# Attention scores from four 64x64 products without the masked quarter, tokens' halves exchanged in every second head pair

## The chip, the cores and the metric

The kernel runs on one core of one Trainium2 chip. The metric is the device time of one launch in microseconds (us), less is better. Three runs of the kernel before took 798.5, 800.56 and 801.65 us.

## What is computed

A linear attention with decay, then two feed-forward layers. Per batch and head the attention goes over the tokens t in order:

```
cur   = (u * k_t) outer v_t
y_t   = r_t . (state + cur)
state = w * state + k_t outer v_t
```

There are 4 batches, 8 heads, 768 tokens and 48 numbers per head. Its output (3072 tokens of 384) goes through a layer of 8 experts, of which each token uses the one with the greatest gate, and through a gated layer: `(silu(x @ w_gate) * (x @ w_val)) @ w_out` with 1536 inner columns. All is fp32.

## The kernel before, in words

The attention works on 24 tiles of 128 tokens, six tiles to a batch (a sequence). Inside a tile the decay is divided out: with powers of w, `rdT` = r times w to the token's number and `kdT` = k divided by w to that number, both with the head's numbers on the partitions, and the *scores* are their product. Two heads share the 128 partitions, 64 each (48 used); so 8 heads are 4 pairs, counted by `q`, with `j` for the head in the pair.

The steps of a tile, and who does them:

- `scaled_k` (L454): GpSimd makes `ck` (k times u times r, L470 and L471), `kdT` (L473) and `kdc` (k decayed to the end of the tile, L475; not for the last tile of a sequence). In the first three tiles VectorE makes `ck` (L467, L468).
- `scaled_r` (L477): VectorE makes `rdT` (L484); for the last two tiles GpSimd does (L482). The loads of the tile three further on are issued here, on the queue of the sync engine (L356, L357, L361).
- `bonus` (L491): VectorE sums `ck` to `cb` (L496), and ScalarE writes for each head a diagonal matrix `dsb` with `cb` on the diagonal, from the identity (L500).
- `scores` (L503): TensorE makes for each head a 128x128 product (keys by queries) with 64 rows of the array (L513); the two heads of a pair use the two halves of the rows, and their results go to two PSUM buffers. VectorE copies them into `dsb`, only where the key comes before the query, by a mask (L517, one instruction for four heads).
- `state` (L525): TensorE makes the tile's addition to the state (L535), VectorE adds it (L545).
- `outputs` (L553): TensorE multiplies `v` by `dsb` (L561) and the state by `rdT` (L569; not for the first tile of a sequence); ScalarE copies the sum (L574).
- `rows_out` (L604): TensorE turns the result to one token per partition (L126, 64x64 products), ScalarE copies it, and a DMA stores it.

The order of the instructions is written out by hand for TensorE, VectorE, ScalarE and GpSimd (L624 on): in the round of tile i come the scores of i, then state and outputs of i-1 and the keys of i+2, then the rows of i-2. The routing of tokens to experts is cut into small steps of VectorE, which `advance` puts between the others (L583); its TensorE steps are issued where `advance(TENSOR)` stands.

Ahead of the loop, `powers` (L389) fills TensorE with five warm-up products `wu` (L397), all into one PSUM buffer, makes the powers of w on VectorE, and on ScalarE the four decay tables `we` (L411), which TensorE turns (L414) and ScalarE copies to `wk_tok` (L415); `kdc` needs that. `tables` (L417) has GpSimd clear the rest of the scratch buffer `yd_all` (L420), from which `carve` cuts the inputs' places. In GpSimd's order the keys of the tiles follow each other without anything else but these and, near the end, the splitting of expert weights (L1079).

After the attention the expert layer and the gated layer follow, mostly on TensorE; the change does not touch them. `sequential` (L779) is a slow branch for other decays than those that occur here; it is not taken.

Of the kernel before, what the change touches and what calls it, by code (L numbers as in the profile page):

```python
# [9 lines left out]
F32 = mybir.dt.float32  # L10
# [10 lines left out]
P = 128  # L21
# [17 lines left out]
def moe_kernel(ctx, tc, cst, small, tok, tr, u, w1, w2, m_gate, m_val, m_out, out):  # L39
# [281 lines left out]
    with ExitStack() as actx:  # L321
# [48 lines left out]
        load(0)  # L370
        nc.sync.dma_start(out=u_tok, in_=u.rearrange("(o h) d -> o h d", o=1).to_broadcast([P, H, D]))
        nc.sync.dma_start(out=cs, in_=cst)
        for i in range(1, NIO):
            load(i)
            load_v(i - 1)
# [13 lines left out]
        def powers():  # L389
            nc.vector.memset(ones, 1.0)  # L390
            nc.vector.memset(pw[:, :, 0:1], 1.0)
            for t in kdc_b:
                nc.gpsimd.memset(t[:, :, D:], 0.0)

            for i in range(WARM):
                wu = ps_m.tile([P, 512], F32, name="wu", tag="m")
                nc.tensor.matmul(  # L397
                    wu, lhsT=ones, rhs=ones.rearrange("p (o t) -> p o t", o=1).to_broadcast([P, 4, P]), start=True, stop=True
                )
            nc.vector.tensor_scalar(out=wc, in0=wp, scalar1=DECAY_MIN, scalar2=DECAY_MAX, op0=ALU.max, op1=ALU.min)  # L400
            for q in range(NP):
                nc.vector.tensor_tensor_scan(
                    out=pw[:, q, 1:], data0=wc[:, q : q + 1].to_broadcast([P, P]), data1=ones,
                    initial=1.0, op0=ALU.mult, op1=ALU.mult,
                )
            nc.scalar.copy(wr_ps, wrT)

            we = apool.tile([P, NP, P], F32, name="we", tag="yT")
            for q in range(NP):
                nc.vector.reciprocal(wkT[:, q, :], pw[:, q, 1:])  # L410
                nc.scalar.mul(we[:, q, :], wkT[:, q, :], pw[:, q, P : P + 1])  # L411
            pst = ps_m.tile([P, NP, P], F32, name="pst", tag="m")
            for q in range(NP):
                nc.tensor.transpose(pst[:, q, :], we[:, q, :], ident)  # L414
            nc.scalar.copy(wk_tok, pst.rearrange("p q (j d) -> p (q j) d", j=2)[:, :, 0:D])  # L415
# [23 lines left out]
                )  # L439
            nc.gpsimd.tensor_copy(unit[:, :, D:], wg[:, :, 0:G])  # L440

        S = {}

        def inputs(i):
            t = io[i % NIO]
# [45 lines left out]
        def bonus(i):  # L491
            if i >= NTILE:
                return
            r_t, k_t, rT, kT, rdT, kdT, ck, kdc = S[i]
            cb = apool.tile([P, H], F32, name="cb")
            nc.vector.reduce_sum(cb, ck, axis=AX.X)  # L496

            dsb = apool.tile([P, H, P], F32, name="dsb", bufs=3)
            for h in [*range(0, H, 2), *range(1, H, 2)]:
                nc.scalar.mul(dsb[:, h, :], ident, cb[:, h : h + 1])  # L500
            S[i] = rdT, kdT, kdc, dsb, heads(io_v[i % NV], 64)

        def scores(i):  # L503
            rdT, kdT, kdc, dsb, v_t = S[i]

            if i == 1:
                both = ps_x.tile([P, 2, NP, P], F32, name="pss01", tag="x")
                pss = [both[:, j] for j in range(2)]
            else:
                pss = [ps_s.tile([P, NP, P], F32, name=f"pss{j}", tag="s") for j in range(2)]  # L510
            for q, j in itertools.product(range(NP), range(2)):
                p0 = 64 * j
                nc.tensor.matmul(  # L513
                    pss[j][:, q, :], lhsT=kdT[p0 : p0 + 64, q, :], rhs=rdT[p0 : p0 + 64, q, :], start=True, stop=True
                )
            for j in range(2):
                nc.vector.copy_predicated(  # L517
                    dsb.rearrange("p (q j) t -> p q j t", j=2)[:, :, j, :],
                    mask.bitcast(I32).rearrange("p (o t) -> p o t", o=1).to_broadcast([P, NP, P]),
                    pss[j],  # L520
                )
                advance()
                advance()
# [255 lines left out]
    def sequential(c):  # L779
# [11 lines left out]
        with tc.For_i(0, B) as b:  # L791
            nc.vector.memset(st, 0.0)
            with tc.For_i(0, NCH) as ch:
                i = b * NCH + ch
                rk = sq.tile([P, 2, NP, P], F32, name="sq_rk")
                nc.sync.dma_start(
                    out=rk.rearrange("p a q t -> p (a q t)"), in_=tr[bass.ds(i, 1)].rearrange("o p n -> (o p) n")
                )
                yT = sq.tile([P, NP, P], F32, name="sq_y")
                nc.vector.memset(yT, 0.0)  # L800
                with tc.For_i(0, P) as t:
                    kv = sq.tile([P, NP, D], F32, name="sq_kv")
                    for j in range(2):
                        nc.sync.dma_start(
                            out=kv[64 * j : 64 * j + 64],
                            in_=v_d[bass.ds(i, 1), j, bass.ds(t, 1), :, 0:D]
                            .rearrange("o a q d -> (o a) q d").to_broadcast([64, NP, D]),
                        )
                    r_t, k_t = (rk[:, n, :, bass.ds(t, 1)] for n in range(2))
                    nc.vector.tensor_tensor(out=kv, in0=kv, in1=bc(k_t), op=ALU.mult)  # L810
                    cur = sq.tile([P, NP, D], F32, name="sq_cur")
                    nc.vector.tensor_tensor(out=cur, in0=kv, in1=col(up), op=ALU.mult)
                    nc.vector.tensor_tensor(out=cur, in0=cur, in1=st, op=ALU.add)
                    nc.vector.tensor_tensor(out=cur, in0=cur, in1=bc(r_t), op=ALU.mult)
                    psy = ps_m.tile([P, NP], F32, name="sq_psy", tag="m")
                    for q in range(NP):
                        for p0 in (0, 64):
                            nc.tensor.matmul(
                                psy[p0 : p0 + D, q : q + 1], lhsT=cur[p0 : p0 + 64, q, :], rhs=ones[p0 : p0 + 64, :],
                                start=True, stop=True,  # L820
                            )
                    for p0 in (0, 64):
                        pr = slice(p0, p0 + D)
                        nc.vector.tensor_copy(yT[pr, :, bass.ds(t, 1)], psy[pr].rearrange("p (q o) -> p q o", o=1))
                    nc.vector.tensor_tensor(out=st, in0=st, in1=col(wp), op=ALU.mult)
                    nc.vector.tensor_tensor(out=st, in0=st, in1=kv, op=ALU.add)
                for _ in emit(
                    yT, x_d[bass.ds(i * P, P), :], lg[:, bass.ds(i, 1), :].rearrange("p o g -> p (o g)"), sq, ps_y
                ):
                    pass  # L830
# [662 lines left out]
def _layout(inputs):  # L1493
# [7 lines left out]
    def tokens(a, pad=0):  # L1501
        a = a.transpose(0, 2, 1, 3)
        if pad:
            a = np.concatenate([a, np.zeros(a.shape[:3] + (pad,), a.dtype)], axis=3)
        return a.reshape(b * n, P, -1)

    def pair_rows(a, fill):

# [48 lines left out]
```

## Time and profile before

| | |
|---|---|
| median of three runs | 800.56 us (798.5 to 801.65) |
| profiled execution | 798.91 us, its span 797.2 us |
| TensorE busy | 777.5 us, 98% of the span |
| VectorE busy | 498.1 us, 62% |
| ScalarE busy | 346.8 us, 44% |
| GpSimd busy | 220.2 us, 28% |

The span runs from the first to the last instruction of the profiled execution. The attention lies in the first 116 us or so. In the rows below PE is TensorE, DVE VectorE, ACT ScalarE, POOL GpSimd and SP the sync engine, whose rows here are issues of DMAs; L513 is line 513 of the kernel. Times count from the start of the span. An fp32 product of TensorE is recorded as two MATMUL records.

### The profile page before, as it was taken

Reading aid. Unit: us, or ns where it says so; the run is one execution under the profiler, and the core shown is the slowest. Engines: PE = TensorE matmul, PEld = TensorE weight load, DVE = VectorE, ACT = ScalarE, POOL = GpSimd, SP = SyncE. Lnnn points to the kernel's source line nnn. Section 1 sums busy time; section 2 is a strip of 40 time slices with the busy share of each in tenths; the row PEclk is TensorE's granted clock in tenths of the full one; section 3 lists DMA queues with packets and bytes.
Section 4 is the critical chain, followed back from the end, with each engine's and each line's share of the span. In section 5 each row is a group of like instructions: output and inputs, shape, how many; then the busy total and the mean of one; then the engine's idle time right before and its main releaser. Section 6 shows DMA issues by size and latency. Waiting matters only on the chain.

```text
span 797.2 us, 15589 instructions
## 1 busy us (share of the span) xinstructions
PE 777.5 (98%) x5982; PEld 713.3 (89%) x5983; DVE 498.1 (62%) x1041; ACT 346.8 (44%) x785; POOL 220.2 (28%) x213
## 2 busy tenths in 40 slices
PE   8989998999999999999999999999999999999997
PEld 4878888899999999988888888888888888899997
DVE  7889976889999899787553335334433543344543
ACT  5878873656656656654432223222212221122322
POOL 6999986545233322120002000100200020001000
PEclk9999999999999999999999999999999999999999
DMA  8999974867877784564201000000100000000000
GB/s 321 307 336 339 303 268 142 289 199 220 253 239 238 248 246 144 159 191 140 89 14 40 1 0 14 40 1 1 44 9 1 7 40 1 1 8 40 1 21 24
DMA packets 61860, 99.28 MB, mean 125 GB/s; under 512 B 5461, under 2 KB 48105, under 8 KB 61776
## 3 DMA queue, kind: packets, MB, share of 16 engines
q1 hardware_dynamic: 58320, 88.34, 34.0%
q0 software_dynamic: 3456, 9.85, 3.6%
q8 instruction: 49, 0.80, 0.4%
q14 instruction: 35, 0.29, 0.1%
HBM read 81.64 MB, written 16.53 MB: 123 GB/s over the span
## 4 chain that ended last, share of the span: by engine, by line
issue 54%; PE 29%; POOL 8%; DVE 5%; DMA 1%; ACT 1%; POOLq 0%; SPq 0%; DVEq 0%; ACTq 0%
PE ph L1209 10%; PE py L1209 9%; POOL out_dram L1381 2%; PE pss L513 1%; PE psy L561 1%; POOL kdT L473 1%; POOL kdc L475 1%; PE psy L569 1%; POOL ck L470 1%; PE pya L1209 1%; PE wu L397 1%; POOL ck L471 1%; DMA rw<-m 1%; PE pt L1176 1%; PE pha L1209 1%
## 5 line engine op out<-in xcount | busy, mean ns | idle before, releaser
L1405 PE MATMUL pg<-x,wh 128*128 128x512 f32 (+1 forms) x504 | 146.6, 359 | 0.0
L1410 DVE TENSOR_TENSOR hv<-pg,hv 128x512 f32<-128x512 f32 (+1 forms) x84 | 51.6, 615 | 141.5 <-ACT hv L1409 141.4
L1405 PE MATMUL pv<-x,wh 128*128 128x512 f32 (+1 forms) x504 | 137.7, 358 | 0.0
L1381 POOL DMA_INDIRECT out_dram<-ot,tokd x24 | 24.9, 1038 | 407.1 <-DVE ot L1380 403.4
L1409 ACT ACTIVATE hv<-pg 128x512 f32<-128x512 f32 (+1 forms) x84 | 45.0, 536 | 158.5 <-PE pg L1405 158.1
L968 ACT CAST hh<-hv 128x512 fp32r<-128x512 f32 (+1 forms) x84 | 47.0, 560 | 136.7 <-DVE hv L1411 136.7
L1405 PEld LDWEIGHTS pv<-x,wh 128*128 128x128 f32 x504 | 89.9, 188 | 13.9
L1405 PEld LDWEIGHTS pg<-x,wh 128*128 128x128 f32 x504 | 90.2, 188 | 11.3
L1372 PE MATMUL po<-wh,hl 128*128 128x384 f32 x288 | 97.1, 338 | 0.0
L1372 PE MATMUL po<-wl,hh 128*128 128x384 f32 x288 | 96.8, 336 | 0.0
L1372 PE MATMUL po<-wh,hh 128*128 128x384 f32 x288 | 96.8, 336 | 0.0
L1405 PE MATMUL pg<-x,wl 128*128 128x512 f32 (+1 forms) x252 | 90.3, 358 | 0.0
L1405 PE MATMUL pv<-x,wl 128*128 128x512 f32 (+1 forms) x252 | 90.3, 358 | 0.0
L1209 PE MATMUL ph<-x,w1h 128*128 128x416 f32 (+6 forms) x336 | 87.5, 341 | 0.0
L1209 PE MATMUL py<-h,w2h 128*128 128x416 f32 (+6 forms) x336 | 82.4, 341 | 0.0
L969 DVE TENSOR_TENSOR hl<-hv,hh 128x512 fp32r<-128x512 f32 (+1 forms) x84 | 51.7, 616 | 43.6 <-ACT hh L968 43.3
L1411 DVE TENSOR_TENSOR hv<-pv,hv 128x512 f32<-128x512 f32 (+1 forms) x84 | 51.7, 615 | 38.5 <-PE pv L1405 37.9
L500 ACT ACTIVATE dsb<-cs,cb 128x128 f32<-128x128 f32 x192 | 58.7, 390 | 16.2 <-DVE cb L496 16.0
L1209 PEld LDWEIGHTS ph<-x,w1h 128*128 128x128 f32 x336 | 61.5, 188 | 0.2
L1209 PEld LDWEIGHTS py<-h,w2h 128*128 128x128 f32 x336 | 60.7, 188 | 0.5 <-DVE h L1229 0.3
L1050 POOL TENSOR_TENSOR low<-low,exw 128x384 f32<-128x384 f32 x30 | 32.9, 1098 | 97.7 <-DVE exw L1046 74.2
L1209 PE MATMUL ph<-x,w1l 128*128 128x416 f32 (+6 forms) x168 | 58.4, 348 | 0.7 <-DVE h L1229 0.7
(237 smaller groups left out, 1498.9 us busy)
## 6 DMA issues: line engine op xcount, KB each, us to landing
r<-in_w_dram SPq DMA_DIRECT2D x64, 384.0 KB
yd_all<-in_tr_dram SPq DMA_DIRECT2D x24, 512.0 KB
yd_all<-in_tok_dram SPq DMA_DIRECT2D x24, 384.0 KB
rw<-m SPq DMA_DIRECT2D x36, 192.0 KB
yd_all<-in_tok_dram SPq DMA_DIRECT2D x24, 256.0 KB
m<-ab SPq DMA_DIRECT2D x30, 192.0 KB
x_d<-xt SPq DMA_DIRECT2D x24, 192.0 KB
cva<-in_w_gate_dram SPq DMA_DIRECT2D x10, 384.0 KB
```

What stands on the lines that cost most here:

```text
L397: nc.tensor.matmul(wu, lhsT=ones, rhs=ones.rearrange("p (o t) -> p o t", o=1).to_broadcast([P, 4, P]), start=True, stop=True)
L500: nc.scalar.mul(dsb[:, h, :], ident, cb[:, h : h + 1])
L968: first = nc.scalar.copy(hi, src)
L969: second = nc.vector.tensor_tensor(out=lo, in0=src, in1=hi.bitcast(F32), op=ALU.subtract)
L1050: nc.gpsimd.tensor_tensor(out=low, in0=low, in1=ex.bitcast(F32), op=ALU.mult)
L1209: nc.tensor.matmul(dst[:, 0:n], lhsT=a, rhs=b, start=start and t == 0, stop=stop and t == 2)
L1372: mm = nc.tensor.matmul(po[t], lhsT=a[:, t * P : (t + 1) * P], rhs=bb, start=(f == 0 and j == 0), stop=(f == KF2 - 1 and j == 2))
L1381: st = nc.gpsimd.indirect_dma_start(out=out[:, :], out_offset=bass.IndirectOffsetOnAxis(ap=tokd[:, i : i + 1].bitcast(U32), axis=0), in_=o ...
L1405: nc.tensor.matmul(dst, lhsT=a[:, fs], rhs=bb[:, q, :], start=(q == 0 and j == 0), stop=(q == KD - 1 and j == 2))
L1409: nc.scalar.activation(hv, pg, AF.Sigmoid)
L1410: nc.vector.tensor_tensor(out=hv, in0=pg, in1=hv, op=ALU.mult)
L1411: nc.vector.tensor_tensor(out=hv, in0=pv, in1=hv, op=ALU.mult)
```

## The change

The scores of a head are made from two products instead of one, with keys and queries cut in halves of 64 tokens: the first 64 keys by all 128 queries, and the last 64 keys by the last 64 queries. The last 64 keys by the first 64 queries, all masked, are left out. In every second pair of heads the halves of the keys change places among the partitions: the first 64 keys stand on partitions 64 to 127. The host lays out r, k and v of these pairs so, the decay table `we` of these pairs is written in two pieces, and the identity and the mask have a second form, loaded by three DMAs behind the constants. The score buffers are the same ones all the time, and the first four warm-up products write them.

```diff
         nc.sync.dma_start(out=cs, in_=cst)
+        both = carve(4 * P).rearrange("p (s m t) -> p m s t", s=2, t=P)
+        for to, of in ((slice(0, P),) * 2, (slice(0, 64), slice(64, P)), (slice(64, P), slice(0, 64))):
+            nc.sync.dma_start(
+                out=both[to, :, int(to != of), :], in_=cst[of, 0 : 2 * P].rearrange("p (m t) -> p m t", t=P)
+            )
+        idents, masks = both[:, 0], both[:, 1]
         for i in range(1, NIO):
             load(i)
...
+            pss_b.append([ps_s.tile([P, NP, P], F32, name=f"pss{j}", tag="s") for j in range(2)])
+            both = ps_x.tile([P, 2, NP, P], F32, name="pss01", tag="x")
+            pss_b.append([both[:, j] for j in range(2)])
             for i in range(WARM):
-                wu = ps_m.tile([P, 512], F32, name="wu", tag="m")
+                wu = pss_b[i // 2][i % 2].rearrange("p q t -> p (q t)") if i < 4 else ps_m.tile([P, 512], F32, name="wu", tag="m")
...
-                nc.scalar.mul(we[:, q, :], wkT[:, q, :], pw[:, q, P : P + 1])
+                for a in range(1 + q % 2):
+                    to, of = (slice(0, P),) * 2 if q % 2 == 0 else (slice(64 * a, 64 * a + 64), slice(64 - 64 * a, P - 64 * a))
+                    nc.scalar.mul(we[:, q, to], wkT[:, q, of], pw[:, q, P : P + 1])
...
-                nc.scalar.mul(dsb[:, h, :], ident, cb[:, h : h + 1])
+                nc.scalar.mul(dsb[:, h, :], idents[:, h // 2 % 2], cb[:, h : h + 1])
...
-            if i == 1:
-                both = ps_x.tile([P, 2, NP, P], F32, name="pss01", tag="x")
-                pss = [both[:, j] for j in range(2)]
-            else:
-                pss = [ps_s.tile([P, NP, P], F32, name=f"pss{j}", tag="s") for j in range(2)]
-            for q, j in itertools.product(range(NP), range(2)):
-                p0 = 64 * j
+            pss = pss_b[i == 1]
+            for q, a, j in itertools.product(range(NP), range(2), range(2)):
+                pr, at = slice(64 * j, 64 * j + 64), 64 * (a ^ q % 2)
                 nc.tensor.matmul(
-                    pss[j][:, q, :], lhsT=kdT[p0 : p0 + 64, q, :], rhs=rdT[p0 : p0 + 64, q, :], start=True, stop=True
+                    pss[j][at : at + 64, q, 64 * a :], lhsT=kdT[pr, q, 64 * a : 64 * a + 64], rhs=rdT[pr, q, 64 * a :],
+                    start=True, stop=True,
                 )
             for j in range(2):
                 nc.vector.copy_predicated(
-                    dsb.rearrange("p (q j) t -> p q j t", j=2)[:, :, j, :],
-                    mask.bitcast(I32).rearrange("p (o t) -> p o t", o=1).to_broadcast([P, NP, P]),
-                    pss[j],
+                    dsb.rearrange("p (o s j) t -> p o s j t", s=2, j=2)[:, :, :, j, :],
+                    masks.bitcast(I32).rearrange("p (o s) t -> p o s t", o=1).to_broadcast([P, NP // 2, 2, P]),
+                    pss[j].rearrange("p (o s) t -> p o s t", s=2),
                 )
...
-        return a.reshape(b * n, P, -1)
+        a = a.reshape(b * n, P, h // 4, 2, 2, -1)
+        return np.stack([a[:, :, :, 0], np.roll(a[:, :, :, 1], 64, axis=1)], axis=3).reshape(b * n, P, -1)
```

The branch `sequential` is rewritten to read the exchanged values.

## Rows read from the trace of the kernel before

**Rows 1.** Busy us (and instructions) of the engines by stretch, then clock, DMA, GB/s.

```profile
core 0: us, PE busy (x) PEld busy (x) DVE busy (x) ACT busy (x) POOL busy (x), PEclk, DMA share, GB/s
11.17:109.06 97.89, 90.19 (x2020) 80.83 (x2016) 86.72 (x243) 80.15 (x255) 95.67 (x94) 0.98 0.95 335
...
180.00:200.00 20.00, 20.00 (x110) 19.64 (x109) 19.55 (x35) 13.27 (x27) 9.66 (x9) 1.00 0.77 225
```

**Rows 2.** Waits of POOL from 11 to 109.1 us: total, times, longest.

```profile
POOL kdc L475 <- ACT yd_all L415: 2.6, 1, 2.6
POOL ck L470 <- DMA yd_all<-in_tok_dram: 0.3, 1, 0.3
```

**Rows 3.** Groups of POOL from 11 to 109.1 us: busy us, mean ns, idle before.

```profile
L473 POOL TENSOR_TENSOR kdT<-yd_all 128x512 f32<-128x512 f32 x23 | 29.4, 1277 | 0.0
...
L475 POOL TENSOR_TENSOR kdc<-yd_all 128x384 f32<-128x384 f32 x20 | 20.3, 1017 | 2.6 <-ACT yd_all L415 2.6
...
L420 POOL MEMSET yd_all<- 128x860 f32 x1 | 0.8, 821 | 0.0
```

**Rows 4.** POOL in order of time: start, us, instruction; tiles 6 and 12.

```profile
32.92 1.28 POOL L473 TENSOR_TENSOR kdT<-yd_all 128x512 f32<-128x512 f32 x1
...
57.41 1.27 POOL L473 TENSOR_TENSOR kdT<-yd_all 128x512 f32<-128x512 f32 x1
```

**Rows 5.** PE in order of time over one tile, from scores to scores.

```profile
27.73 1.16 PE L513 MATMUL pss<-rdT,kdT 64*128 64x128 f32 x16
28.82 0.69 PE L535 MATMUL pskv<-yd_all,kdc 128*64 128x64 f32 x16
29.33 1.05 PE L561 MATMUL psy<-dsb,yd_all 128*64 128x128 f32 x16
30.31 0.98 PE L569 MATMUL psy<-rdT,st 64*64 64x128 f32 x14
...
31.13 0.73 PE L126 MATMUL psx<-unit,yT 64*64 64x64 f32 x30
31.79 1.16 PE L513 MATMUL pss<-rdT,kdT 64*128 64x128 f32 x16
```

**Rows 6.** POOL and PE in order of time where the last scores start.

```profile
107.80 1.20 POOL L482 TENSOR_TENSOR rdT<-yd_all 128x512 f32<-128x512 f32 x1
...
109.06 1.16 PE L513 MATMUL pss<-rdT,kdT 64*128 64x128 f32 x16
```

**Rows 7.** Chain of waits from 1 to 13 us: start, us, what.

```profile
3.22 2.09 PE wu L397 x2
...
9.95 0.64 PE pst L414 x4
...
11.17 1.13 POOL kdc L475
```

**Rows 8.** Start of the kernel: ACT, DVE and POOL in order of time, and one stretch.

```profile
7.54 0.40 ACT L411 ACTIVATE we<-yd_all 128x128 f32<-128x128 f32 x1 [0.41 <-DVE yd_all L410]
...
10.88 0.57 DVE L467 TENSOR_TENSOR bank<-yd_all 128x384 f32<-128x384 f32 x1 [0.75 <-DMA yd_all<-in_tok_dram]
...
13.49 1.01 POOL L475 TENSOR_TENSOR kdc<-yd_all 128x384 f32<-128x384 f32 x1
...
7.00:20.00 13.00, 10.35 (x105) 7.12 (x104) 10.22 (x18) 7.86 (x27) 10.16 (x14) 0.87 1.03 403
```

**Rows 9.** Group of the masked copy: busy us, mean ns, idle before.

```profile
L517 DVE COPY_PREDICATED dsb<-cs,pss 128x512 f32<-128x512 int32 x48 | 33.0, 739 | 3.2 <-PE pss L513 3.2
```

**Rows 10.** Chain of waits from 55 to 120 us, its shares by line.

```profile
by line: PE pss L513 17.0%; PE psy L561 15.8%; PE psy L569 13.5%; PE psx L126 10.1%; PE pskv L535 8.7%; DVE dsb L517 6.6%; DVE p_oh L209 4.3%; issue 4.3%; DVE yd_all L133 2.1%; DVE sel L216 1.8%; PE bank L220 1.6%; DVE x L969 1.6%; DVE bank
```

**Rows 11.** Two stretches as in rows 1, and PE in order of time around the first.

```profile
14.40:17.80 3.40, 3.40 (x42) 2.85 (x40) 3.37 (x7) 1.38 (x5) 3.28 (x6) 0.51 1.04 396
57.00:60.40 3.40, 1.88 (x42) 1.69 (x41) 3.40 (x11) 1.25 (x4) 3.40 (x4) 1.00 0.86 286
...
13.59 0.60 PE L513 MATMUL pss<-rdT,kdT 64*128 64x128 f32 x6 [1.91 <-POOL kdT L473]
...
15.75 1.92 PE L561 MATMUL psy<-dsb,yd_all 128*64 128x128 f32 x16
```

More of the change, by code (lines that the diff above doesn't have):

```diff
@@ L440, in units @@
             nc.gpsimd.tensor_copy(unit[:, :, D:], wg[:, :, 0:G])
-        S = {}
+        S, pss_b = {}, []
         def inputs(i):
@@ L800, in sequential @@
                 nc.vector.memset(yT, 0.0)
[L801 to L816, printed above, removed]
-                        for p0 in (0, 64):
[L818 to L826, printed above, removed]
@@ new lines, in sequential @@
+                for a in range(2):
+                    with tc.For_i(0, 64) as s:
+                        t = s + 64 * a
+                        kv = sq.tile([P, NP, D], F32, name="sq_kv")
+                        for j, o in itertools.product(range(2), range(2)):
+                            nc.sync.dma_start(
+                                out=kv[64 * j : 64 * j + 64, o::2, :],
+                                in_=v_d[bass.ds(i, 1), j, bass.ds(s + 64 * (a ^ o), 1), o::2, 0:D]
+                                .rearrange("o a q d -> (o a) q d").to_broadcast([64, NP // 2, D]),
+                            )
+                        r_t, k_t = (rk[:, n, :, bass.ds(t, 1)] for n in range(2))
+                        nc.vector.tensor_tensor(out=kv, in0=kv, in1=bc(k_t), op=ALU.mult)
+                        cur = sq.tile([P, NP, D], F32, name="sq_cur")
+                        nc.vector.tensor_tensor(out=cur, in0=kv, in1=col(up), op=ALU.mult)
+                        nc.vector.tensor_tensor(out=cur, in0=cur, in1=st, op=ALU.add)
+                        nc.vector.tensor_tensor(out=cur, in0=cur, in1=bc(r_t), op=ALU.mult)
+                        psy = ps_m.tile([P, NP], F32, name="sq_psy", tag="m")
+                        for q in range(NP):
+                            for p0 in (0, 64):
+                                nc.tensor.matmul(
+                                    psy[p0 : p0 + D, q : q + 1], lhsT=cur[p0 : p0 + 64, q, :], rhs=ones[p0 : p0 + 64, :],
+                                    start=True, stop=True,
+                                )
+                        for p0 in (0, 64):
+                            pr = slice(p0, p0 + D)
+                            nc.vector.tensor_copy(yT[pr, :, bass.ds(t, 1)], psy[pr].rearrange("p (q o) -> p q o", o=1))
+                        nc.vector.tensor_tensor(out=st, in0=st, in1=col(wp), op=ALU.mult)
+                        nc.vector.tensor_tensor(out=st, in0=st, in1=kv, op=ALU.add)
```

## Prediction

> **What bounds the kernel now.** I read the stretch of the attention first, because only there does the change touch anything that runs. Busy time by engine [rows 1]: from 11.17 to 109.06 us GpSimd works 95.67 of 97.89 us, VectorE 86.72, TensorE 90.19 (its ends are modelled, so this overstates it), and the DMA engines are busy 0.95 of the time. From 180 us on TensorE works 20.00 of 20 us. So a microsecond won at the end of the attention is carried through to the end, and the question is which engine ends the attention. The list of GpSimd's waits in that stretch has two entries [rows 2]: 2.6 us at the very start, for the table of decays that ScalarE copies, and 0.3 us for one load. Everything else is its own work; its two costliest groups [rows 3] are 23 products for the keys of the scores at 1.277 us and 20 for the keys of the state at 1.017. The line of time shows the pace [rows 4]: from the keys of tile 6 at 32.92 us to those of tile 12 at 57.41 us are 24.49 us for six tiles, 4.08 us each, back to back.
>
> TensorE's line of time over one tile [rows 5] shows the same pace with no hole: scores at 27.73, next scores at 31.79, 4.06 us. But that is a full tile. The first tile of a sequence has no product with the state (L569, 0.82 us), the last has no L535 (0.51), so six tiles are 6 x 4.06 - 1.33 = 23.0 us on TensorE against 24.49 on GpSimd. GpSimd never waits for TensorE. So GpSimd is the floor of this stretch, and TensorE runs just under it. At the end of the stretch GpSimd's last decayed rows (107.80 us, 1.20 long) release the last scores at 109.06 [rows 6].
>
> **The change, part by part.** *Scores.* Now a tile has 16 TensorE records (two to a product), two beside each other, so 8 steps of 128 columns: 1.09 us from L513 to L535 [rows 5]. After it there are 32 records on four quarters of the array. A step of 128 columns costs 0.82/8 = 0.10 us (L569, 30.31 to 31.13, the same 64x64 form); a step of 64 columns on four quarters costs 0.66/8 = 0.08 (L126, 31.13 to 31.79) [rows 5]. Each quarter gets 4 long and 4 short steps: 0.40 + 0.32 = 0.72 us, 0.37 less. If the quarters of unequal length did not overlap by columns, it would be 8 long and 8 short steps, 1.46 us, 0.37 more. L126 runs the four quarters together, so I take 0.72.
>
> The Trainium skill, TensorE: Matmul & The Clock Gate, Part 3 ("The mechanism"), speaks against the full figure: matmuls start and end strictly in program order. By that the short products of one pair hold up the long ones of the next, which use the same quarters, and a tile would come to about 8 long steps, 0.82 us; the sum below would lose 0.1 us. The trace of before has no unequal products on which to see it.
>
> What is it worth? Over 23 tiles 0.37 us is hidden behind GpSimd: TensorE is merely done earlier and waits. Only the last scores, released by GpSimd at 109.06, lie on the path: **-0.3 us** (ends -0.37 and +0.37). The doubled records (768 become 1536) cost nothing beyond this; what hides them is GpSimd's 4.08 us per tile, and without that cover the cost is the upper end.
>
> *Warm-up products.* Five of them run at the start, each waiting for the one before, since all write the same buffer. The chain [rows 7] gives 2.09 us for the two records of the second one (3.22), and it leads on to the transpose (9.95) that makes the table for which GpSimd waits until 11.17. In the change the first four write four different score buffers, and none waits. What they need without the wait: 8 steps of 0.10 per 128 columns is 0.80 us for two records of 512 columns at full clock, some 1.6 to 1.7 at half, against 2.09. Three waits of about 0.4 and one of about 0.3 go; part of the won time is at the half clock and is worth less. I take **-1.0 us** for the start of GpSimd's chain. Ends: 0 (they follow each other as before), and -1.5, because ScalarE's last input of the transpose, now done at 7.94 (7.54 + 0.40), will be there at some 8.4 [rows 8].
>
> *Two more ScalarE instructions* in the table of decays, at most 0.40 each like the present four [rows 8]; one of them is the last of the row. They end before the warm-up does, and it hides them; without that cover they cost 0.4.
>
> *Three loads ahead of tile 1.* They carry 128 x 2 x 128 numbers twice, 262 KB; at the 403 GB/s of this stretch [rows 8] that is 0.65 us, and the DMA engines are full (share 1.03). On the sync queue everything behind them (the loads of tiles 1 and 2, the first values) is issued three issues later. VectorE waits for tile 1 until 10.88 already [rows 8]; that becomes 11.5, and its work for tiles 0 and 1 slides with it. GpSimd needs tile 1's keys at 13.49 [rows 8], two microseconds after that. But it will be a microsecond earlier and the loads 0.65 later; the DMA share of 0.95 leaves little to catch up with, and GpSimd already waits 0.3 for a load [rows 2]. So part of the 1.0 is given back as waits for loads: **+0.5 us** (ends 0 and +1.5, all that was won; if nothing was won at the start, +0.65).
>
> *The clearing of the scratch room.* GpSimd clears what is left of the scratch buffer, 860 columns in 0.821 us [rows 3]. The two new tables take 512 of them, so 348 are left: 0.33 us, **-0.5 us** in the saturated chain. Ends -0.5 and 0.
>
> *VectorE's masked copies*, 48 at 739 ns [rows 9], keep their 512 elements; mask and destination now have three free dimensions instead of two. I take 0; a price is in the rivals. *ScalarE's diagonals* read another table of the same shape: nothing. The loop for wide decays lies in a branch that is not taken.
>
> **The sum.** -1.0 + 0.5 - 0.5 - 0.3 = -1.3 us. The profiled execution took 798.91 us, of which 797.2 are the span and 1.7 lie around it, so it would become 797.6. The three runs shown have a median of 800.56, 1.65 above the profiled one; against that median I forecast **799.3 us**. A change under 0.5%, 4 us, can't be told from none here.
>
> **The rivals.** *A: TensorE is the bound, and every tile gains.* For it: the chain of waits from 55 to 120 us names the scores first, with 17.0% [rows 10]. Then 24 x 0.37 = 8.9 us go, 791.7. Against it: GpSimd's work does not shrink by this and it has no holes to fill [rows 2, 3]; TensorE follows it, it does not feed it. 6%.
>
> *B: VectorE becomes the bound (slower).* Place: the masked copy L517. VectorE has 97.89 - 86.72 = 11.2 us free in the stretch [rows 1], 0.23 us for each of 48 copies. From 0.97 us a copy on VectorE sets the pace, and from 1.06 us the loss passes 4 us. If the third dimension halves the rate, 1.48 us: 48 x 0.74 - 11.2 = 24 us, 825. For it: no row shows this form. Against it: the number of elements is the same. 4%.
>
> *C: the quarters do not overlap (the change doesn't do what it says).* At 1.46 us TensorE's full tile becomes 4.43 us and six tiles 6 x 4.43 - 1.33 = 25.25, against GpSimd's 24.49 [rows 4, 5]: 0.76 for each of four sequences and 0.37 for the last scores, +3.4, 804.0. It decides from scores of about 1.33 us. Against it: L126 overlaps. 4%.
>
> *D: the clock falls.* Between 14.4 and 17.8 us the granted clock was 0.51 on the mean, so the lower level, 1.2 GHz [rows 11], after TensorE had waited 1.91 us for the keys; L561 then took 1.92 us against 1.05 [rows 5, 11]. TensorE will wait more often now. For a fall near 106 us, with nothing to hide it, half of 3.4 us is lost, 1.7: 801.0. Against it: between 57 and 60.4 us TensorE worked only 1.88 of 3.40 us and the clock stayed at 1.00 [rows 11]. 6%.
>
> **How the numbers follow.** My case has 80%. Its lower end takes all gains: -1.5 - 0.5 - 0.37 = -2.4; its upper end none, with the late loads and the worse scores: 0.65 + 0.37 = +1.0. To both come 1.6 us, half the spread of the runs shown (798.5 to 801.65): 796.6 to 803.2, which takes in D as well. A, B and C lie outside. Faster by over 0.5% is A and the edge of my case, 0.07; slower by over 0.5% is B and, with scatter, part of C, 0.06; the rest, 0.87, is no difference.
>
> **What would show it.** Right: GpSimd's wait at the start ends near 10.2 us instead of 11.17; its chain still has no wait for TensorE, 4.08 us per tile; its clearing shows 348 columns and 0.33 us; TensorE gets waits for GpSimd's keys or rows that it does not have now; scores to L535 take 0.7 to 0.85 us; the last scores start near 108. Wrong: a mean of L517 over 0.97 us, scores over 1.1 us, GpSimd waiting for TensorE, waits for loads of more than 2 us in all, or a tile of GpSimd shorter than 4.08 us, which would make rival A possible.

## The result: slower by 0.85%, and the profile after

The kernel after took 807.33 us (median of six runs, 805.07 to 808.27); the kernel before, run beside it, 799.88 (six runs, 798.35 to 801.65). The ratio is 1.0085, with an interval of 1.0068 to 1.0102: about 7 us slower. The forecast was 799.3 us, with a range up to 803.2; it missed on the slow side. The profiled execution after took 805.59 us, its span 803.7, against 798.91 and 797.2 before.

**Where the time went.** The expert stage begins with the products of `pha`. Their first one, in order of time, stands at 118.04 us before and at 125.46 after (the first fence is before, the second after):

```profile
118.04 0.36 PE L1209 MATMUL pha<-x,w1l 128*128 128x256 f32 x1 [0.38 <-ACT lh L128]
```

```profile
125.46 0.36 PE L1219 MATMUL pha<-x,w1l 128*128 128x256 f32 x1 [0.37 <-ACT lh L128]
```

From there to the end of the span are 679.2 us before and 678.2 after. So all of the loss, 7.4 us, arises in the attention. Busy time by stretch in the kernel after, first the stretch of [rows 1], then three stretches of the attention (columns as in [rows 1]):

```profile
11.17:109.06 97.89, 81.80 (x2217) 73.18 (x2219) 82.58 (x230) 74.92 (x238) 91.51 (x91) 0.95 0.92 322
...
40.00:60.00 20.00, 15.69 (x481) 14.08 (x474) 15.95 (x48) 15.35 (x48) 19.61 (x20) 1.00 0.94 319
...
80.00:100.00 20.00, 17.80 (x501) 16.22 (x502) 16.00 (x43) 14.70 (x47) 16.82 (x17) 0.91 0.81 277
100.00:120.00 20.00, 15.06 (x385) 12.84 (x383) 13.97 (x51) 11.80 (x35) 14.88 (x13) 1.00 0.83 281
```

Every engine works less in the stretch from 11.17 to 109.06 us: TensorE 81.80 us for 90.19 before, and GpSimd 91.51 for 95.67. From 40 to 60 us GpSimd is still full, as forecast, while TensorE idles over 4 us; from 80 us on GpSimd has holes too. No engine is full all the way to the end, so none of them alone sets the pace; something delays them all.

**The waits of TensorE** from 20 to 118 us tell what. Before, there is one row of "issue" (the first fence); after, all of these rows and the longest of another kind stand in the second (us in total, times, longest):

```profile
PE psx L126 <- issue: 0.8, 2, 0.5
```

```profile
PE psx L126 <- issue: 5.6, 3, 2.9
PE pss L520 <- issue: 2.5, 5, 1.1
PE psy L569 <- issue: 2.2, 2, 2.0
PE psy L577 <- issue: 2.2, 2, 1.4
PE psy L569 <- ACT yT L582: 1.7, 2, 1.4
PE bank L178 <- issue: 0.5, 1, 0.5
...
```

"issue" means that the engine waited for nothing that the profile shows. That is 5.6 + 2.5 + 2.2 + 2.2 + 0.5 = 13.0 us after, against 0.8 before. The waits fall in the middle of groups whose data are all there. The longest, in order of time:

```profile
77.58 0.47 PEld L126 LDWEIGHTS psx<-unit,yT 64*64 64x64 f32 x13
...
77.69 0.50 PE L126 MATMUL psx<-unit,yT 64*64 64x64 f32 x11
...
78.54 1.26 POOL L484 TENSOR_TENSOR kdT<-yd_all 128x512 f32<-128x512 f32 x1
...
81.06 0.42 PEld L126 LDWEIGHTS psx<-unit,yT 64*64 64x64 f32 x19 [3.02 <-issue]
81.07 0.56 PE L126 MATMUL psx<-unit,yT 64*64 64x64 f32 x19 [2.88 <-issue]
```

The 32 weight loads of a tile's rows are cut after 13; the other 19 come 3 us later, with the same `yT` and the same `unit`. Their data are there, so what is missing must be the instructions themselves; the DMA queues bear this out. What the DMA queues carried from 78.69 to 79.65 us (packets, MB, share of 16 engines):

```profile
q1 hardware_dynamic: 166, 0.36, 102.2%
q8 instruction: 1, 0.02, 6.1%
```

Queue q8 carries instructions in packets of 16 KB; the count below shows that TensorE's are among them. This packet's record begins at 78.70 us and lasts 0.94; TensorE goes on at 81.07, 1.43 us after its end. In the 0.5 us ahead of it and in the 1.4 us behind it the queue view has no q8 packet, only data, with the DMA engines full. Packets that begin at 42.11, 47.40, 57.52, 100.20, 105.72 and 111.90 us are followed in the same way, 1.3 to 1.7 us after their end, by the ends of waits of 1.62, 1.15, 1.08, 2.01, 0.83 and 1.36 us. So end 11 of the 13 "issue" waits between 20 and 118 us; the other two are of 0.24 and 0.27 us. Over the whole execution q8 carries this (packets, MB, share):

```profile
q8 instruction: 52, 0.85, 0.4%
```

It was 49 packets and 0.80 MB before. The Trainium skill, TensorE: Matmul & The Clock Gate, Part 2 ("Step-by-step: what each phase is for"), speaks of the 64-byte MATMUL instruction. The trace agrees in size, for matmuls and weight loads together: the page counts 6366 matmuls and 6367 weight loads after against 5982 and 5983, 768 more in all, and 768 times 64 bytes is three packets of 16 KB.

**How the rest answers to the rows before.** GpSimd's work, its wait at the start, one tile of TensorE and VectorE's masked copies:

```profile
L484 POOL TENSOR_TENSOR kdT<-yd_all 128x512 f32<-128x512 f32 x23 | 29.3, 1275 | 0.0
L481 POOL TENSOR_TENSOR ck<-yd_all 128x384 f32<-128x384 f32 x21 | 21.1, 1006 | 2.9 <-DMA yd_all<-in_tok_dram 2.9
...
L486 POOL TENSOR_TENSOR kdc<-yd_all 128x384 f32<-128x384 f32 x20 | 20.8, 1040 | 2.5 <-PE pskv L543 1.3 <-ACT yd_all L426 1.2
...
L431 POOL MEMSET yd_all<- 128x348 f32 x1 | 0.4, 385 | 0.0
```

```profile
10.01 1.00 POOL L486 TENSOR_TENSOR kdc<-yd_all 128x384 f32<-128x384 f32 x1 [1.18 <-ACT yd_all L426]
```

```profile
24.85 0.90 PE L520 MATMUL pss<-rdT,kdT 64*64 64x128 f32 x32
25.68 0.69 PE L543 MATMUL pskv<-yd_all,kdc 128*64 128x64 f32 x16
```

```profile
L525 DVE COPY_PREDICATED dsb<-yd_all,pss 128x512 f32<-128x512 int32 x43 | 29.6, 733 | 9.8 <-PE pss L520 6.6 <-ACT xt L130 2.0 <-ACT lh L128 0.5
```

The scores take 25.68 - 24.85 = 0.83 us up to L543, where they took 1.09 [rows 5]. The start wait of GpSimd ends 1.16 us earlier [rows 7]. But GpSimd now waits 2.9 us for loads instead of 0.3, 1.7 of them from 79.8 us on, and 1.3 us for TensorE's state products (L543), which read the buffer `kdc` that it wants to write; that it never did [rows 2].

The last scores start at 115.27 us, 6.2 later than in [rows 6]. From 100 to 126 us the chain of waits has 20.9% "issue" and no piece of GpSimd at all. There the stalls lie on the path themselves:

```profile
99.95 0.54 PE psy L569 x9
100.49 2.01 issue
102.50 0.65 PE psy L569 x7
...
112.43 0.69 PE psy L577 x9
113.11 1.36 issue
114.47 0.54 PE psy L577 x6
```

**When it is lost** can be read from GpSimd's keys. Those of tile 17 (78.54 us after, shown above) start 0.10 us earlier than before; those of tile 23, the last, start 2.68 us later. The first two rows are before, the third is after:

```profile
78.64 1.27 POOL L473 TENSOR_TENSOR kdT<-yd_all 128x512 f32<-128x512 f32 x1
...
104.79 1.27 POOL L473 TENSOR_TENSOR kdT<-yd_all 128x512 f32<-128x512 f32 x1
```

```profile
107.47 1.27 POOL L484 TENSOR_TENSOR kdT<-yd_all 128x512 f32<-128x512 f32 x1
```

So the waits that end before 70 us, 4.8 of the 13.0, cost GpSimd's pace nothing, and up to there the added loads, the tables and the exchange have not set it back either. The 8.2 us of waits from 78.19 us on come together with the whole loss of 7.4.

Last, the granted clock. Near the start its stretch at 0.50 (second row), the lower level of 1.2 GHz, is longer than the one in [rows 11], 6.83 us for 3.40; by the keys of tile 17 that has cost GpSimd nothing. And the clock fell once more, right after the 2.9 us stall (first row):

```profile
81.64:85.05 3.41, 3.41 (x63) 3.26 (x65) 2.25 (x7) 3.04 (x10) 2.46 (x3) 0.50 0.58 169
13.37:20.20 6.83, 6.21 (x104) 5.64 (x106) 6.80 (x13) 3.59 (x12) 5.82 (x9) 0.50 1.04 398
```

### The profile page after: what moved, and what is told of

The parts are those of the page before. It is cut to its first block, busy times and chain, and to the rows that moved or that the text cites. A ratio compares the mean times of both kernels' runs of the same rounds, so it can differ in the third digit from the quotient of the medians.

```text
span 803.7 us, 16363 instructions
## 1 busy us (share of the span) xinstructions
PE 773.3 (96%) x6366; PEld 710.6 (88%) x6367; DVE 496.5 (62%) x1041; ACT 347.8 (43%) x787; POOL 220.3 (27%) x213
## 4 chain that ended last, share of the span: by engine, by line
issue 56%; PE 24%; DVE 8%; DMA 5%; POOL 4%; ACT 2%; SPq 1%; POOLq 0%; ACTq 0%; DVEq 0%
PE ph L1219 5%; PE py L1219 5%; PE psy L569 2%; POOL out_dram L1391 2%; PE psy L577 2%; PE pss L520 2%; PE pskv L543 1%; PE psx L126 1%; DMA m<-ab 1%; PE pya L1219 1%; DMA m<-x 1%; DVE ab L1063 1%; DMA rw<-m 1%; PE pha L1219 1%; DVE w2l L1089 1%
## 5 line engine op out<-in xcount | busy, mean ns | idle before, releaser
L511 ACT ACTIVATE dsb<-yd_all,cb 128x128 f32<-128x128 f32 x192 | 58.8, 393 | 12.4 <-DVE cb L507 12.2
```

The lines of the kernel that those rows point to most:

```text
L511: nc.scalar.mul(dsb[:, h, :], idents[:, h // 2 % 2], cb[:, h : h + 1])
```

## The experiments

The theory after this reading, called **program** below: TensorE has 768 more instructions and gets through them sooner, its next pieces of program queue behind data in full DMA engines, and it stalls. The rivals: the additional loads, tables and exchanged halves cost; or keeping the score buffers costs; or the form of the products does. All runs in one table. "Ratio" is to the kernel before of the same session; "issue" is TensorE's wait for nothing that the profile shows from 20 to 118 us; q8 the packets of program; the last column is the first product of `pha`. The last three columns are of the one profiled execution, which need not be a middle one: those of e4 (800.42 us, median 798.25) and e12 (805.58, median 802.96) are the longest of their runs, that of e13 (800.89, median 801.96) is among the shortest.

| run | ratio (interval) | issue, us | q8 | attention ends, us |
|---|---|---|---|---|
| before | 1 | 0.8 | 49 | 118.04 |
| after | 1.0085 (1.0068 to 1.0102) | 13.0 | 52 | 125.46 |
| after, again (e14) | 1.0082 (1.0061 to 1.0104) | 14.6 | 52 | 127.19 |
| after, rows by 8 (e1) | 1.0046 (1.0029 to 1.0064) | 0.5 | 49 | 123.35 |
| before, rows by 8 (e2) | 1.0083 (1.0054 to 1.0112) | 0 | 46 | 123.84 |
| before, scores split (e3) | 1.0157 (1.0129 to 1.0186) | 1.5 | 52 | 136.23 |
| before, three loads (e4) | 0.9994 (0.9978 to 1.0010) | 5.5 | 49 | 120.88 |
| after, fewer v loads (e5) | | 1.7 | | 117.14 |
| before, fewer v loads (e6) | | 0 | | 116.61 |
| after, rounded rows (e7) | 1.0004 (0.9991 to 1.0018) | 1.0 | 47 | 120.04 |
| before, empty instructions (e8) | 1.0002 (0.9990 to 1.0015) | 2.5 | 49 | 119.17 |
| before, spread warm-up (e9) | 0.9988 (0.9968 to 1.0009) | 6.6 | 49 | 122.66 |
| before, rounded rows (e10) | 0.9969 (0.9945 to 0.9994) | 0 | 44 | 117.44 |
| after, half split (e11) | 1.0076 (1.0052 to 1.0100) | 0.7 | 50 | 125.71 |
| before, quarters (e12) | 1.0052 (1.0032 to 1.0072) | 10.0 | 52 | 126.37 |
| before, quarters in odd tiles (e13) | 1.0054 (1.0034 to 1.0074) | 3.4 | 50 | 119.30 |

In the session of e9 to e11 the kernel before itself took 803.66 us (798.82 to 806.60), in all others 797.85 to 799.88.

The table can also be read execution by execution. In the eight with all loads, the rows of x by 16 products, and in each tile either whole or quartered scores (before, e8, e13, e4, e9, e12, after, e14), the waits are 0.8, 2.5, 3.4, 5.5, 6.6, 10.0, 13.0 and 14.6 us, and the attention ends at 118.04, 119.17, 119.30, 120.88, 122.66, 126.37, 125.46 and 127.19: nearly in step, whichever kernel it is.

**e1 and e2: the rows of x in half as many products.**

```diff
-        for q, (j, k) in itertools.product(range(NP), ((0, 0), (1, 1), (0, 1), (1, 0))):
-            pr, ts = slice(64 * j, 64 * j + 64), slice(64 * k, 64 * k + 64)
-            nc.tensor.matmul(psx[ts, j, q, :], lhsT=yT[pr, q, ts], rhs=unit[pr, q, :], start=True, stop=True)
+        for q, j in itertools.product(range(NP), range(2)):
+            pr = slice(64 * j, 64 * j + 64)
+            nc.tensor.matmul(psx[:, j, q, :], lhsT=yT[pr, q, :], rhs=unit[pr, q, :], start=True, stop=True)
```

> The changed kernel, but the rows of a tile (L126) are made by 8 products of 64x128 instead of 16 of 64x64, so TensorE's program has as many products per tile as before the change (48 instead of 56). Theory code: TensorE runs through its program faster than the next piece of it arrives, while the DMA engines are full; its waits for nothing that the profile shows, 13.0 us in the attention of the changed kernel and 0.8 before, fall under 2 us, and the time falls to 797 to 800.5 us. Theory loads (the three loads ahead of tile 1 delay what follows): the time stays at 805 to 808, GpSimd's waits for loads at about 2.9 us. Theory array (the 64x64 products themselves or the clock): 805 to 808.

> The kernel before with the rows of a tile made by 8 products instead of 16: 40 products per tile instead of 48. Theory code: the kernel before waits only 0.8 us for its program, so little is there to win: 798.5 to 801. The other theories say the same; a loss of over 1 us would price the form 64x128 in place of 64x64 for the rows.

The waits went (0.5 and 0 us), as the theory has it, but neither time came (e1 802.69 us, e2 804.71): both kernels pay for the form, 128 columns of weights for 64 streamed ones. In e2 the weight loads, grouped by form from 60 to 80 us (busy us, mean ns):

```profile
L126 PEld LDWEIGHTS psx<-unit,yT 64*128 64x128 f32 x75 | 4.6, 188 | 0.7 <-issue 0.5 <-ACT dsb L500 0.2
...
L569 PEld LDWEIGHTS psy<-rdT,st 64*64 64x64 f32 x48 | 2.5, 133 | 0.5 <-issue 0.3 <-DVE dsb L517 0.2
```

From the rows' first record to the next scores it is 0.94 us in e2 (64.71 to 65.65 us), and before it was 0.66 [rows 5], with twice as many products. The longer weight loads fit that; that they alone set the pace is not shown. TensorE became the bound in e2 (20.00 us busy of 20 between 40 and 60 us). The Trainium skill, TensorE: Matmul & The Clock Gate, Part 2 ("Step-by-step: what each phase is for"), has this rule: the time of a weight load scales with its columns, not with its rows. The two rows agree in direction (188 ns for 128 columns, 133 for 64); both have 64 rows, so they say nothing on that half of the rule. What the two runs show together: the same edit costs 0.8% before and gains about 0.4% after. They do not give the size of the stalls.

**e3: additional instructions in the kernel before**, each score product in two, by halves of the queries.

```diff
-                nc.tensor.matmul(
-                    pss[j][:, q, :], lhsT=kdT[p0 : p0 + 64, q, :], rhs=rdT[p0 : p0 + 64, q, :], start=True, stop=True
-                )
+                for ts in (slice(0, 64), slice(64, P)):
+                    nc.tensor.matmul(
+                        pss[j][:, q, ts], lhsT=kdT[p0 : p0 + 64, q, :], rhs=rdT[p0 : p0 + 64, q, ts], start=True, stop=True
+                    )
```

> The kernel before with each product of the scores split by queries into two of 64 columns: 56 products per tile as in the changed kernel, but the form 64x128, the masked quarter, the layout and the loads of before; TensorE's work grows by about 0.05 us a tile. Theory code: waits of 8 to 14 us in TensorE's stream and 804 to 809 us. Theory loads: 799 to 801. Theory array: 799 to 801.5.

Longer by more than forecast (811.71 us), and not by stalls: each weight of 128 columns is loaded twice, and the scores take a median of 1.98 us up to the next group instead of 1.09, not 0.05 more. It waits 1.5 us for its program although it has as many instructions as after. So the number alone does not do it. Two reasons are possible, and the run does not separate them: TensorE, held up by its products, needs the next piece later; and the data queue's share from 20 to 118 us is 81.7% here, not 88.2%.

**e4: the three loads and the smaller clearing alone**, in the kernel before.

```diff
+        both = carve(4 * P).rearrange("p (s m t) -> p m s t", s=2, t=P)
+        for to, of in ((slice(0, P),) * 2, (slice(0, 64), slice(64, P)), (slice(64, P), slice(0, 64))):
+            nc.sync.dma_start(
+                out=both[to, :, int(to != of), :], in_=cst[of, 0 : 2 * P].rearrange("p (m t) -> p m t", t=P)
+            )
```

> The kernel before with the three loads of the second identity and mask behind the constants, unused (and 512 columns less for GpSimd to clear). Theory code: 799.5 to 801.5, no new wait of TensorE. Theory loads: 804 to 808, with GpSimd waiting for loads about 2.9 us. Theory array: 800.

No change in the median. Yet its profiled execution, the longest of twelve, has 5.5 us of the same waits:

```profile
PE pskv L540 <- issue: 3.7, 2, 2.0
...
PE psx L126 <- issue: 1.0, 1, 1.0
PE psy L566 <- issue: 0.8, 2, 0.5
```

So the stalls are no new thing of this change. They were not free here either: the attention of this execution ends 2.84 us later than in that of before, although GpSimd's last keys start 0.64 us earlier (104.15 us for 104.79), and one stall of 2.01 us lies on the chain that ends last, from 98 to 122 us:

```profile
101.67 2.01 issue
```

**e5 and e6: the same programs with less DMA.** From tile 4 on no values are loaded, so the outputs are computed from old ones; the tokens then crowd on few experts and a branch for that runs, which adds some 280 us behind the attention (so the 796 to 800 us expected of e6 could not come). Only the attention can be compared.

```diff
-            if i < NTILE:
+            if i < NV:
```

> The changed kernel without the loads of v from tile 4 on (these tiles work on the v of earlier tiles): 256 of the 1344 KB that a tile moves are gone, and TensorE's program is unchanged. To be held against the kernel before with the same edit. Theory code: the pieces of the program come sooner, TensorE's 13.0 us of waits for nothing shown fall under 4 us, and the time is within 1.5 us of that of the kernel before with the same edit. Theory start-and-layout (the warm-up, the exchanged tables or the clock make it slower): 5 to 8 us above it.

> The kernel before without the loads of v from tile 4 on. It is the partner of the changed kernel with this edit; GpSimd sets the pace, so 796 to 800 us by every theory.

Of the whole time these two tell nothing. Of the attention they tell most. From 20 to 118 us the data queue's share falls to 76.8% in e5, from 88.2% after, and the same products, 32 instructions more a tile than before, now wait 1.7 us instead of 13.0. The attention ends at 117.14 against 116.61: 0.5 us between the two programs where it was 7.4, with the loads, tables and exchange of the change in place. GpSimd's waits for tokens fall too, from 2.9 us to 1.5; e7 tells the two apart. The largest row of this kind that e5's waits still have:

```profile
PE psx L126 <- issue: 0.9, 2, 0.7
```

**e7 and e10: the same loads with fewer instructions.** The rows by 8 products as in e1, but in the rounded 32-bit format, so that x is rounded there; one product is then one weight load and one matmul. A tile has 48 instructions less than after.

```diff
-    unit = const.tile([P, NP, 64], F32, name="unit")
+    unit = const.tile([P, NP, 64], F32R, name="unit")
...
-            yT = apool.tile([P, NP, P], F32, name="yT")
+            yT = apool.tile([P, NP, P], F32R, name="yT")
...
```

> The changed kernel with the rows of a tile made by 8 products of the short fp32r form instead of 16 of fp32 (x is rounded): 16 records less each of loads and products twice over, so a tile's program is about 176 instructions instead of 224 (192 before the change), and each array step is cheaper. Theory code: TensorE's waits for nothing shown fall under 1.5 us and the time to 796.5 to 799.5, below the kernel before. Theory start-and-layout: 803 to 808.

> The partner of the run with the rounded rows, on the kernel before: the rows of x by 8 products with operands in the rounded 32-bit format, 64x128 each, in place of 16 of 64x64, so x is rounded there. Theory: the kernel before waits 0.8 us for its program and is bound by GpSimd, so 40 products less per tile than after give nothing: 796.5 to 799.5 us. Rival (the rounded rows are a gain of their own of some 9 us, which only covered the change's loss in the earlier run): 789 to 793 us.

With the change in place, its loads, tables and exchange included, 47 packets of program instead of 52 bring the time back to that of before (797.99 us, though not below it, as forecast). What is left of the waits in e7:

```profile
PE pskv L545 <- issue: 0.8, 1, 0.8
...
PE pss L522 <- issue: 0.2, 1, 0.2
```

GpSimd still waits 2.2 us for its loads there (2.9 after), so those waits were not the loss. TensorE has less work in e7 too, so the run does not separate fewer instructions from more time to spare. The partner e10 is not the 1% faster that the rival needs, but 0.3%: with the rounded rows the change still seems to cost about 1.0004 / 0.9969, 0.35%, in two different sessions. It is also the only kernel of the study that is clearly faster than before, by less than the 0.5% that counts, and for a rounding. (Its expectation says 40 products less per tile than after; it has 40 per tile, after has 56.)

**e8: empty instructions.** 32 a tile were put behind the score products of the kernel before.

```diff
+                for _ in range(4):
+                    nc.tensor.nop(nofuse=True)
```

> The kernel before with 32 empty instructions per tile in TensorE's program, among the scores: as many instructions per tile as in the changed kernel, with no work in the array. Theory code: waits for nothing shown of 8 us or more between 20 and 118 us, 803 to 809 us. Theory start-and-layout: 798 to 801, if an empty instruction costs under 10 ns.

No change, and no test: the program still has 49 packets, where 768 more instructions of 64 bytes would have made it 52.

**e9: the warm-up alone.** The kernel before with the score buffers kept and the first four warm-up products spread over them.

```diff
+            pss_b.append([ps_s.tile([P, NP, P], F32, name=f"pss{j}", tag="s") for j in range(2)])
+            both = ps_x.tile([P, 2, NP, P], F32, name="pss01", tag="x")
+            pss_b.append([both[:, j] for j in range(2)])
             for i in range(WARM):
-                wu = ps_m.tile([P, 512], F32, name="wu", tag="m")
+                wu = pss_b[i // 2][i % 2].rearrange("p q t -> p (q t)") if i < 4 else ps_m.tile([P, 512], F32, name="wu", tag="m")
```

> The kernel before with one part of the change alone: the first four warm-up products go into the four score buffers, which are allocated once; the scores stay 8 products of 128 columns. Theory (the loss comes from TensorE's program arriving late, and needs the additional score products): the start gains about a microsecond and loses it at the loads, 797.0 to 799.5 us, no more than 0.8 us of TensorE's waits for nothing that the profile shows. Rival (keeping the score buffers for good, or starting earlier into the full loads, is what costs): 802 us or more, with GpSimd's waits on the tokens' loads near 3 us.

No change against the kernel before beside it, whose time in that session is as long. The expectation of 0.8 us of waits failed: 6.6 us. How many the kernel before had in that session isn't known; no profile of it was taken there.

**e11: half of the additional instructions, by whole products for the pairs that are not exchanged.**

```diff
-            for q, a, j in itertools.product(range(NP), range(2), range(2)):
-                pr, at = slice(64 * j, 64 * j + 64), 64 * (a ^ q % 2)
...
+            for q in range(NP):
+                for a, j in itertools.product(range(1 + q % 2), range(2)):
+                    pr, at = slice(64 * j, 64 * j + 64), 64 * (a ^ q % 2)
+                    ks, to = (slice(64 * a, 64 * a + 64), slice(at, at + 64)) if q % 2 else (slice(0, P),) * 2
...
```

> The kernel after with its loads, tables and exchanged halves as they are, but the scores of the pairs that are not exchanged by one product of 128x128 each head instead of two by quarters: 12 score products a tile instead of 16 (8 before), so half of the additional instructions. Theory (program): TensorE's waits for nothing that the profile shows fall from 13.0 us to between 2 and 8 us, and the time to 799 to 804 us. Rival (the loss comes from the additional loads, the exchanged halves or the earlier start): 805 to 808 us as after.

The time fits the rival, the waits (0.7 us) do not. Order of time shows why: products of two shapes in turn take longer than products of one shape.

```profile
46.07 1.65 PE L522 MATMUL pss<-rdT,kdT 64*128 64x128 f32 x24
47.65 0.69 PE L544 MATMUL pskv<-yd_all,kdc 128*64 128x64 f32 x16
```

The scores take 1.58 us up to the next group, against 0.83 after and 1.09 before (half of each would be 0.96), and TensorE is the bound (20.00 us busy of 20 between 40 and 60). So this run tells nothing of how the stalls grow with the number of instructions.

**e12, e13 and e14: the additional products alone.** e12 is e9 with the quarters of the scores in every tile, in the old layout: no loads, no tables, no exchange. e13 has them in odd tiles only. e14 is the kernel after beside them.

```diff
-            for q, j in itertools.product(range(NP), range(2)):
-                p0 = 64 * j
+            for q, a, j in itertools.product(range(NP), range(2), range(2)):
+                pr, at = slice(64 * j, 64 * j + 64), 64 * a
                 nc.tensor.matmul(
-                    pss[j][:, q, :], lhsT=kdT[p0 : p0 + 64, q, :], rhs=rdT[p0 : p0 + 64, q, :], start=True, stop=True
+                    pss[j][at : at + 64, q, at:], lhsT=kdT[pr, q, at : at + 64], rhs=rdT[pr, q, at:], start=True, stop=True
                 )
```

> The kernel before with the score buffers kept for good (as in the run with the spread warm-up) and the scores of every tile by quarters of 64 keys without the masked one, but with no halves exchanged: no additional loads, no tables, the old layout of the records. 16 score products a tile as after. Theory (the additional TensorE instructions are late from memory and need nothing else of the change): waits of TensorE for nothing that the profile shows of 6 us or more, attention as late as after, the time 4 to 9 us over the kernel before and within 3 us of the kernel after on the same chip. Rival (the additional loads, the tables or the exchanged halves cost): the time within 2 us of the kernel before.

> The same, but only in the odd tiles; the even ones keep 8 score products of 128x128. Half of the additional instructions (192 products of 384). Theory: waits between those of the kernel before and those of the run with quarters in every tile, the time 1 to 6 us over the kernel before. Rival (the loads or the exchange): within 2 us of the kernel before. If the run with all quarters is slow and this one is as slow as that, the waits are no matter of the number of instructions but of where single pieces arrive.

> The kernel after, unchanged, on the chip of the two runs beside it. Both theories: 1.005 to 1.010 of the kernel before. If the kernel after is no slower here, the loss belongs to single chips or runs, and the runs beside it say nothing on it.

Medians: before 798.34, e12 802.96, e13 801.96, after 805.43 us. The waits of e12, then of e13:

```profile
PE psx L126 <- issue: 6.2, 4, 2.6
PE psy L560 <- issue: 2.4, 1, 2.4
...
PE pss L512 <- issue: 1.2, 1, 1.2
...
PE psy L568 <- issue: 0.2, 1, 0.2
```

```profile
PE pss L513 <- issue: 1.8, 1, 1.8
...
PE psx L126 <- issue: 0.9, 3, 0.3
...
PE psy L575 <- issue: 0.5, 1, 0.5
PE psy L567 <- issue: 0.2, 1, 0.2
```

The quarters alone bring the stalls and 4.6 of the 7.1 us; e9, which lacks only the quarters, was no slower than the kernel before beside it. Half of them in e13 bring 3.6 us, as much as all of them within the noise (1.0054 for 1.0052). By the criterion put on record with e13, the waits then go less by the number of instructions than by where single pieces arrive. The waits of the two profiles, 10.0 and 3.4 us, do not decide it, as one is of e12's longest execution and the other of one of e13's shortest. In e14 a wait of 2.17 us that ends at 62.70 already sets GpSimd back, so how long the stalls stay covered differs too.

The 2.5 us by which e12 stays below after are uncertain, since the two intervals overlap. After's keys up to tile 17 and the 0.5 us between e5 and e6 speak against a cost of the loads, tables or exchange by themselves; that the shorter scores (0.83 us for e12's 1.02) make TensorE need its program sooner is possible and was not tried.

## Why the prediction was wrong

- **The step that failed** is "The doubled records (768 become 1536) cost nothing beyond this; what hides them is GpSimd's 4.08 us per tile". The records were priced by the time of the array alone, and bringing in 768 more weight loads and matmuls was put at nothing. They come in packets through the same DMA engines, whose share of 0.95 stood in [rows 1] and was used only for the loads. The runs put 13.0 and 14.6 us of stalls in its place (after and e14), and 4.6 us of time for the additional products alone (e12).
- **Its cover failed too.** GpSimd's 4.08 us per tile did hide 4.8 us of stalls, up to the keys of tile 17. The 8.2 us from 78.19 us on, the first of them 2.88 us long and followed by 3.41 us at the lower clock, were not hidden: GpSimd then waits for TensorE itself, and at the end of the attention TensorE's stalls lie on the path, where no GpSimd work covers them. Why the cover held for the first and not for the second was not tried; e4 lost at the end as well.
- **GpSimd as the floor** was right for the kernel before, and up to 78.5 us after, where its keys keep the times of before within 0.2 us from tile 5 on. "Its chain still has no wait for TensorE" fell with 1.3 us.
- **Scores**: 0.72 us forecast, 0.83 measured, so 0.26 us won and not 0.37. This agrees with what the rule of the Trainium skill cited there gave (TensorE: Matmul & The Clock Gate, Part 3, "The mechanism": program order, 0.82). The exchange does help: in e12, without it, the scores take 26.88 - 25.86 = 1.02 us.
- **Last scores**: they were to start near 108 us and be 0.3 us shorter; they started at 115.27.
- **Warm-up**: -1.0 forecast, 11.17 - 10.01 = 1.16 us measured at GpSimd's wait. **Loads**: +0.5 forecast; GpSimd waits for tokens 0.81 us at 17.82 and 0.38 at 22.48, so all that was won is given back, the upper end of the term. In e4 (the loads alone) and e9 (the warm-up alone) GpSimd has no such wait before 60 us, and neither time moves.
- **Clearing**: forecast 0.33 us, measured 0.385 for 348 columns. Right in GpSimd's order: its keys are 0.27 us later than before ahead of it (24.52 us, tile 4) and 0.15 us earlier behind it (29.48, tile 5). So warm-up, loads and clearing made -0.15 us together, not -1.0, and the stalls then outweighed it.
- **Rival B** is out: the masked copy took 733 ns, as before. **C** is out with 0.83 us. **A** did not come: the scores became shorter and no tile of GpSimd did. **D** came, in another place: the clock fell after a stall, not by the spare time that the shorter scores leave. At half speed, 3.41 us cost TensorE at most 1.7, an estimate; how much of that is in the 7 us was not separated.

## What to carry to other kernels

Where the DMA engines are full, as here at 0.92 to 0.95, count the instructions of a straight-line program as loads: bytes that arrive in pieces, among the data. Their number alone does not give the loss (e3, e13); it matters too how soon TensorE needs a piece and where a stall falls. Splitting a product for the array's sake can win array time and lose more at the program, most of all at the end of a stage, where no other engine's work covers a stall. The sign of it is an "issue" wait in the middle of a group whose operands are long there, ending behind a packet of the instruction queue; the cure, where the precision allows, is fewer instructions (e7) or less traffic (e5).

## What was not expected of the hardware

- TensorE waits for its program up to 2.9 us at a time while the DMA engines are busy 0.9 of the time. Each 16 KB packet lasts 0.88 to 1.53 us (18 of them after, from 20 to 118 us), and in 11 of 13 waits there TensorE goes on 1.3 to 1.7 us after the end of one. With the data queue at 76.8% instead of 88.2% the waits fall from 13.0 to 1.7 us.
- These waits differ from execution to execution in nearly equal programs: 0.8, 2.5, 5.5 and 6.6 us in the kernel before, e8, e4 and e9, all with 49 packets; the ends of the attention go with them.
- Mixed shapes of products cost time: whole and quartered score products in turn take 1.58 us, while all whole ones take 1.09 and all quartered ones 0.83.
- Half as many products can take longer: the rows of x by 8 products with 128 columns of weights and 64 streamed ones take 0.94 us for 0.66 and cost 0.8% of the kernel before.
